# Loading each input tensor of a sequence by one 1.2 MB transfer instead of six 192 KB transfers, in a fused attention and feed-forward kernel

## The chip, the cores and the metric

The kernel runs on one core of a Trainium2 chip. The metric is device time in microseconds (us) of a whole execution, as the median of the runs. The profile is one further execution; its span (first to last instruction) is about 2 us shorter than the time.

Names: TensorE (in the profile PE, and PEld for its weight loads), VectorE (DVE), ScalarE (ACT), GpSimd (POOL), and SyncE (SP), whose queue issues every DMA of this kernel. "L420" is a line of the kernel; the same statement has another number in each variant, so go by the tile names.

## The reference, cut to what matters

```python
# q, k, v, f_logit: (4 sequences, 8 heads, 768 tokens, 48), float32
f = 1 / (1 + exp(-f_logit))
for t in range(768):                       # state: 48 x 48 per head
    state = f[:, :, t, :, None] * state + einsum('bhd,bhe->bhde', k[:, :, t], v[:, :, t])
    y[:, :, t] = einsum('bhd,bhde->bhe', q[:, :, t], state)
x = y.transpose(0, 2, 1, 3).reshape(3072, 384)
out = (maximum(x @ w_in, 0) ** 2) @ w_out  # w_in 384 x 2048, w_out 2048 x 384
```

Each sequence is cut into 6 chunks of 128 tokens, 24 chunks in all. A token's 48 floats of one head (192 bytes) are contiguous in memory; the next token of the head follows, the next head is 768 tokens away. With tokens on partitions every load is therefore made of runs of 192 bytes.

## The kernel before

A small planner inside the program orders all steps: each has an engine, an assumed duration and what it must follow. The result is one fixed order of instructions on each engine. So an instruction whose data is late holds up everything behind it on its engine, even work that is ready.

```python
IOB = 6                                    # six chunk tiles for each of f, k, q, v
LOADS = [0, 1, 2, "i0", "i1", "i2", "i3", 3, 4, 5, "o0", "o1", "o2", "o3"] + list(range(6, NCH))
UNITS = [(0, 2), (2, 1), (3, 1), (4, 1), (5, 1)] + [(c, 3) for c in range(6, NCH, 3)]
...
def load(i):                               # i: chunk; "i0".. and "o0".. are pieces of w_in, w_out
    b, c = divmod(i, NC)
    for n in ("f", "k", "q", "v"):
        def fn(n=n):
            t = io.tile([C, H, D], F32, tag="io_" + n, name="io_" + n)
            nc.sync.dma_start(t, srcs[n][b].rearrange("h s d -> s h d")[c * C:(c + 1) * C])
            st[n, i] = t
        plan.add(f"{n}{i}", "SP", 1.03, fn, take=["io_" + n], rank=0, land=1.9)
```

What follows a load, for chunk i (cut):

```python
a1   ACT   e = exp(-f);  pz = ln(e + 1)            # needs f
p1   PE    pc = ut x pz                            # sums over tokens
a2   ACT   ep = exp(pc);  en = exp(-pc)
v1   DVE   az = k * ep,  q * en                    # needs k, q
p2   PE    tr = transposes of az;   v2: ts = tr
p3   PE    at = ts x ts;            v3: am = at * ut    (DVE)
vc   POOL  vz = v in bf16                          # needs v
p5   PE    ds = az x vz;  s1 DVE tm = ds (+ sz);  s2 POOL sz = tm * en     # state for chunk i + 1
p4   PE    yp = ts x sz + am x vz;  a3: ys = yp;  p6 PE xp = transposes;  v6: xT = xp
mm1  PE    hp = w_in x xT  per unit of 1 to 3 chunks (UNITS);  hr = relu(hp), hT = hr * hr (ACT, DVE)
mm2  PE    op = hT x w_out;  ob = op;  store from the SP queue
```

The buffers pz and az exist twice, so only two chunks can run ahead of the rest. Units of the feed-forward network (FFN) are three chunks wide from chunk 6 on: the FFN of sequence 1 starts when the attention of chunks 6, 7 and 8 is done.

## Time and profile before

The time was 202.44 us (3 runs, 202.26 to 202.61).

| before, from the profile | value |
|---|---|
| TensorE busy | 179.2 of 199.5 us |
| one 192 KB load, issue to issue in the steady state | 1.03 us |
| first cast of v (chunk 0) | 7.20 us |
| first FFN matmul | 19.67 us |
| first FFN matmul of sequence 1 | 70.29 us |

The page of the kernel before, from its parts 1, 2, 3 and 6. The two digit rows are busy tenths in 40 equal slices of the span, the third row is GB/s; the last lines are DMA issues with count, size and median us to landing.

```profile
PE 179.2 (90%) x1824; PEld 122.0 (61%) x1824; DVE 141.7 (71%) x301; ACT 132.2 (66%) x279; POOL 38.6 (19%) x80
...
PE   0667996698989999999999999999999999999973
...
DMA  6999999999999899999989989910111011111111
GB/s 126 192 196 348 318 177 184 252 384 191 207 188 221 192 190 173 230 186 203 208 166 228 212 167 221 164 39 5 39 40 42 0 43 41 39 39 43 39 54 64
DMA packets 107030, 30.19 MB, mean 151 GB/s; under 512 B 100352, under 2 KB 105472, under 8 KB 107008
...
io_f<-in_f_logit_dram SPq DMA_DIRECT2D x24, 192.0 KB, 4.6
...
wi_f<-in_moe_w_in_dram SPq DMA_DIRECT2D x4, 768.0 KB, 8.6
```

The DMA engines are 80%, mostly 90% and more, busy from slice 1 to slice 25 (counted from 0; to 130 us), at some 190 GB/s wherever q, k, v, f are loaded and at up to 384 GB/s in the slices with weights, whose runs are 1.5 to 2 KB. TensorE is at a steady 90% and more only from slice 12 on (60 us). So the early part waits for data and the late part is TensorE's own work.

Stretches of the kernel before: limits and length in us, then busy us (instructions) of PE, PEld, DVE, ACT, POOL, then granted TensorE clock, DMA share, GB/s.

```profile
0.00:71.00 71.00, 56.09 (x692) 42.58 (x693) 55.92 (x114) 46.47 (x93) 19.46 (x45) 1.00 1.05 226
71.00:100.00 29.00, 28.30 (x315) 19.29 (x314) 27.16 (x59) 24.70 (x56) 7.81 (x15) 1.00 1.12 199
100.00:110.00 10.00, 9.72 (x94) 6.25 (x91) 7.78 (x17) 8.12 (x19) 1.98 (x4) 1.00 1.07 197
```

By 71 us TensorE has 56.1 us of work behind it, and is 96% busy from there to the end (123.1 of 128.5 us): at most some 5 us of the time lost before 71 us could be won back.

### The profile page before, as it was taken

To read this page: it belongs to the slowest core of one execution; us is meant where nothing else is said; L and a number is where in the kernel's file an instruction comes from. 1 tells how busy PE (TensorE), PEld (TensorE's weight loads), DVE (VectorE), ACT (ScalarE), POOL (GpSimd) and SP (SyncE) were. 2 spreads that over 40 slices of the span, in tenths; PEclk is the share of its full clock that TensorE was granted. 3 is DMA by queue.
4 is the path that set the end of the run, shared out by engine and by line. 5 is a ranking of instruction groups with operands and counts; after the bars stand their busy time and mean duration, and the time that the engine had idled before them with its cause. 6 is when DMAs were issued, how large, how long until landed. Compare 5 with 4: busy or idle time off the path is not lost.

```text
span 199.5 us, 4771 instructions
## 1 busy us (share of the span) xinstructions
PE 179.2 (90%) x1824; PEld 122.0 (61%) x1824; DVE 141.7 (71%) x301; ACT 132.2 (66%) x279; POOL 38.6 (19%) x80
## 2 busy tenths in 40 slices
PE   0667996698989999999999999999999999999973
PEld 0445785486867666666665666666666665665541
DVE  3569679897799999898987979899755753433200
ACT  4363687696875389769879487787865565555310
POOL 5233011510251323114321211412200200000000
PEclk9999999999999999999999999999999999999999
DMA  6999999999999899999989989910111011111111
GB/s 126 192 196 348 318 177 184 252 384 191 207 188 221 192 190 173 230 186 203 208 166 228 212 167 221 164 39 5 39 40 42 0 43 41 39 39 43 39 54 64
DMA packets 107030, 30.19 MB, mean 151 GB/s; under 512 B 100352, under 2 KB 105472, under 8 KB 107008
## 3 DMA queue, kind: packets, MB, share of 16 engines
q1 hardware_dynamic: 107008, 29.89, 72.5%
q8 instruction: 14, 0.23, 0.5%
q14 instruction: 8, 0.07, 0.1%
HBM read 25.17 MB, written 4.72 MB: 150 GB/s over the span
## 4 chain that ended last, share of the span: by engine, by line
PE 63%; DMA 14%; SPq 10%; ACT 5%; DVE 3%; issue 2%; POOL 1%; DVEq 0%; POOLq 0%; ACTq 0%
PE op L464 26%; PE hp L420 24%; SPq L198 9%; DMA io_f<-in_f_logit_dram 7%; DMA io_v<-in_v_dram 7%; PE tr L312 3%; PE yp L350 3%; PE at L327 2%; PE pc L280 2%; PE xp L364 2%; PE ds L381 1%; ACT pz L270 1%; ACT e L269 1%; ACT ob L474 1%; DVE am L334 1%
## 5 line engine op out<-in xcount | busy, mean ns | idle before, releaser
L420 PE MATMUL hp<-xT,w_in 128*128 128x384 bf16 (+2 forms) x528 | 80.6, 287 | 1.8 <-ACT xT L371 1.3
L464 PE MATMUL op<-w_out,hT 128*128 128x384 bf16 x384 | 77.8, 326 | 2.1 <-ACT ob L474 1.1
L427 ACT ACTIVATE hr<-hp 128x384 bf16<-128x384 f32 (+1 forms) x94 | 47.5, 509 | 23.8 <-PE hp L420 22.7
L420 PEld LDWEIGHTS <-w_in 128*128 128x128 bf16 x528 | 43.3, 99 | 19.7 <-issue 2.1
L436 DVE TENSOR_TENSOR hT<-hr 128x384 bf16<-128x384 bf16 (+1 forms) x91 | 34.3, 378 | 27.5 <-ACT hr L427 26.5
L464 PEld LDWEIGHTS <-hT 128*128 128x128 bf16 x384 | 35.4, 97 | 24.6 <-issue 3.6
L334 DVE TENSOR_TENSOR am<-at,ut 128x512 bf16<-128x512 f32 x48 | 31.7, 682 | 2.2 <-PE at L327 1.9
L398 POOL TENSOR_TENSOR sz<-tm,en 48x192 bf16<-48x192 f32 x40 | 21.9, 549 | 49.6 <-DVE tm L389 30.3
L274 POOL CAST vz<-io_v 128x384 bf16<-128x384 f32 x24 | 13.2, 552 | 66.6 <-DMA io_v<-in_v_dram 39.4
L269 ACT ACTIVATE e<-io_f 128x384 f32<-128x384 f32 x24 | 12.6, 523 | 14.5 <-DMA io_f<-in_f_logit_dram 14.5
L312 PE MATMUL tr<-ident,az 128*128 128x128 bf16 x192 | 16.5, 230 | 2.7 <-DVE az L300 1.6
L300 DVE TENSOR_TENSOR az<-io_k,ep 128x384 bf16<-128x384 f32 x24 | 14.7, 614 | 4.7 <-ACT ep L290 4.6
L429 DVE TENSOR_SCALAR hr<-hp 128x384 bf16<-128x384 f32 (+1 forms) x26 | 15.1, 586 | 2.0 <-PE hp L420 2.0
L434 ACT ACTIVATE hT<-hr 128x384 bf16<-128x384 bf16 (+1 forms) x29 | 15.9, 549 | 0.9 <-DVE hr L429 0.3
L312 PEld LDWEIGHTS <-az 128*128 128x128 bf16 x192 | 12.6, 102 | 6.3 <-DVE az L300 2.4
L474 ACT COPY ob<-op 128x384 f32<-128x384 f32 x18 | 8.6, 477 | 11.4 <-PE op L464 11.3
L280 PE MATMUL pc<-pz,ut 128*128 128x384 bf16 x24 | 8.3, 348 | 8.0 <-ACT pz L270 7.0
L318 DVE COPY ts<-tr 128x1024 bf16<-128x1024 bf16 x20 | 13.7, 684 | 1.6 <-PE tr L312 1.4
L304 DVE TENSOR_TENSOR az<-io_q,en 128x384 bf16<-128x384 f32 x24 | 14.5, 605 | 0.4 <-ACT en L296 0.4
L290 ACT ACTIVATE ep<-pc 128x384 f32<-128x384 f32 x24 | 11.7, 489 | 4.6 <-PE pc L283 4.5
L270 ACT ACTIVATE pz<-e 128x384 bf16<-128x384 f32 x24 | 12.6, 523 | 0.8
L296 ACT ACTIVATE en<-pc 128x388 f32<-128x388 f32 (+1 forms) x24 | 11.9, 494 | 0.0
(40 smaller groups left out, 143.8 us busy)
## 6 DMA issues: line engine op xcount, KB each, us to landing
io_f<-in_f_logit_dram SPq DMA_DIRECT2D x24, 192.0 KB, 4.6
io_k<-in_k_dram SPq DMA_DIRECT2D x24, 192.0 KB, 4.5
io_q<-in_q_dram SPq DMA_DIRECT2D x24, 192.0 KB, 4.5
io_v<-in_v_dram SPq DMA_DIRECT2D x24, 192.0 KB, 4.5
out_dram<-ob SPq DMA_DIRECT2D x24, 192.0 KB, 2.0
wi_f<-in_moe_w_in_dram SPq DMA_DIRECT2D x4, 768.0 KB, 8.6
wo_f<-in_moe_w_out_dram SPq DMA_DIRECT2D x4, 768.0 KB, 7.4
```

Of the source, the lines that this page charges most:

```text
L198: nc.sync.dma_start(t, srcs[n][b].rearrange("h s d -> s h d")[c * C:(c + 1) * C])
L269: nc.scalar.activation(e, st["f", i].rearrange("p h d -> p (h d)"), AFT.Exp, scale=-1.0)
L300: nc.vector.tensor_mul(az[i % 2][:, H:, :D], st["k", i], st["ep", i])
L312: nc.tensor.transpose(tr[:, y, :], a[:, 2 * y:2 * y + 2, :].rearrange("p h d -> p (h d)"), ident)
L334: nc.vector.tensor_mul(t, st["at", i][x], ut4)
L398: nc.gpsimd.tensor_mul(nx[r, :, D * x:D * (x + 1)], st["tm", i][r, :, D * x:D * (x + 1)], st["en", i][r, HD:HD + NP].unsqueeze(2).to_broad ...
L420: nc.tensor.matmul(hp[:, x, :], w_in[:, ks, (f + x) * C:(f + x + 1) * C], xT[:, ks, lo:lo + W], start=(ks == 0), stop=(ks == KS - 1), skip ...
L427: nc.scalar.activation(hr[:, :m, :], st["hp", c0, f][:, :m, :], AFT.Relu)
L429: nc.vector.tensor_scalar_max(hr[:, :m, :], st["hp", c0, f][:, :m, :], 0.0)
L434: nc.scalar.activation(st["hT", g][:, f:f + m, lo:lo + W], hr[:, :m, :], AFT.Square)
L436: nc.vector.tensor_mul(st["hT", g][:, f:f + m, lo:lo + W], hr[:, :m, :], hr[:, :m, :])
L464: nc.tensor.matmul(st["o", i], hT[:, fs, tt * C:(tt + 1) * C], w_out[:, fs, :], start=(fs == 0), stop=(fs == FS - 1))
```

## The change

The intent: 16 large transfers in place of 96 small ones, with fewer issues. Head and chunk strides merge into one dimension (the head stride is six chunk strides), so a whole sequence is one access pattern. All of sequence 0 is loaded, then all weights, then sequences 1, 2, 3. Two large tiles for each tensor take twice the memory of six small ones. The compute engines read slices of the large tiles, with gaps between heads. The planner is told 4.5 us for each large transfer.

```diff
-    IOB = 6
+    IOB = 2
-    LOADS = [0, 1, 2, "i0", "i1", "i2", "i3", 3, 4, 5, "o0", "o1", "o2", "o3"] + list(range(6, NCH))
...
+    LOADS = [0, ("i", 0), ("i", 1), ("i", 2), ("i", 3), ("o", 0), ("o", 1), ("o", 2), ("o", 3), 1, 2, 3]
+    LDUR = 4.5
...
-    def load(i):
-        b, c = divmod(i, NC)
+    def load(b):
         for n in ("f", "k", "q", "v"):
             def fn(n=n):
-                t = io.tile([C, H, D], F32, tag="io_" + n, name="io_" + n)
-                nc.sync.dma_start(t, srcs[n][b].rearrange("h s d -> s h d")[c * C:(c + 1) * C])
-                st[n, i] = t
-            plan.add(f"{n}{i}", "SP", 1.03, fn, take=["io_" + n], rank=0, land=1.9)
+                t = io.tile([C, H, NC, D], F32, tag="io_" + n, name="io_" + n)
+                nc.sync.dma_start(t, srcs[n][b].rearrange("h (c p) d -> p h c d", p=C))
+                for c in range(NC):
+                    st[n, b * NC + c] = t[:, :, c, :]
+            plan.add(f"{n}{b}", "SP", LDUR, fn, take=["io_" + n], rank=0, land=1.9)
...
-        plan.add(f"a1.{i}", "ACT", 1.0, a1, after=[f"f{i}"], take=["pz"], give=[f"io_f:f{i}"])
+        plan.add(f"a1.{i}", "ACT", 1.0, a1, after=[f"f{b}"], take=["pz"])
... (the same for k, q, v; a buffer is given back when its six chunks are used)
```

More of the change, by code (lines that the diff above doesn't have):

```diff
@@ L159 @@
     NCH = B * NC
-    IOB = 6
+    IOB = 2
     WSTB = 4
     HTB = 3
-    LOADS = [0, 1, 2, "i0", "i1", "i2", "i3", 3, 4, 5, "o0", "o1", "o2", "o3"] + list(range(6, NCH))
-    LOADS = [x if isinstance(x, int) else (x[0], int(x[1])) for x in LOADS]
+    LOADS = [0, ("i", 0), ("i", 1), ("i", 2), ("i", 3), ("o", 0), ("o", 1), ("o", 2), ("o", 3), 1, 2, 3]
+    LDUR = 4.5
     UNITS = [(0, 2), (2, 1), (3, 1), (4, 1), (5, 1)] + [(c, 3) for c in range(6, NCH, 3)]
@@ L191 @@
     srcs = {"f": f_logit, "k": k, "q": q, "v": v}
-    def load(i):
-        b, c = divmod(i, NC)
+    def load(b):
         for n in ("f", "k", "q", "v"):
             def fn(n=n):
-                t = io.tile([C, H, D], F32, tag="io_" + n, name="io_" + n)
-                nc.sync.dma_start(t, srcs[n][b].rearrange("h s d -> s h d")[c * C:(c + 1) * C])
-                st[n, i] = t
-            plan.add(f"{n}{i}", "SP", 1.03, fn, take=["io_" + n], rank=0, land=1.9)
+                t = io.tile([C, H, NC, D], F32, tag="io_" + n, name="io_" + n)
[3 more added lines that the diff above has]
+            plan.add(f"{n}{b}", "SP", LDUR, fn, take=["io_" + n], rank=0, land=1.9)
+            use = {"f": "a1", "k": "v1k", "q": "v1q", "v": "vc"}[n]
+            done.append((f"{n}{b}x", [f"{use}.{b * NC + c}" for c in range(NC)], f"io_{n}:{n}{b}"))
+    done = []
     NW = 4
@@ L261, in attention @@
     def attention(i):
-        c = i % NC
+        b, c = divmod(i, NC)
         last = c == NC - 1
@@ L268, in a1 @@
             e = work.tile([C, HD], F32, tag="e", name="e")
-            nc.scalar.activation(e, st["f", i].rearrange("p h d -> p (h d)"), AFT.Exp, scale=-1.0)
+            nc.scalar.activation(e.rearrange("p (h d) -> p h d", d=D), st["f", i], AFT.Exp, scale=-1.0)
             nc.scalar.activation(pz[i % 2][:, :, :D], e.rearrange("p (h d) -> p h d", d=D), AFT.Ln, bias=1.0)
-        plan.add(f"a1.{i}", "ACT", 1.0, a1, after=[f"f{i}"], take=["pz"], give=[f"io_f:f{i}"])
+        plan.add(f"a1.{i}", "ACT", 1.0, a1, after=[f"f{b}"], take=["pz"])
         def vc():
             nc.gpsimd.tensor_copy(vz[i % 3], st["v", i])
-        plan.add(f"vc.{i}", "POOL", 0.52, vc, after=[f"v{i}"], take=["vz"], give=[f"io_v:v{i}"])
+        plan.add(f"vc.{i}", "POOL", 0.52, vc, after=[f"v{b}"], take=["vz"])
         def p1():
@@ L300, in v1k @@
             nc.vector.tensor_mul(az[i % 2][:, H:, :D], st["k", i], st["ep", i])
-        plan.add(f"v1k.{i}", "DVE", 0.5, v1k, after=[f"a2p.{i}", f"k{i}"], take=["az"], give=[f"ep:a2p.{i}", f"io_k:k{i}"])
+        plan.add(f"v1k.{i}", "DVE", 0.5, v1k, after=[f"a2p.{i}", f"k{b}"], take=["az"], give=[f"ep:a2p.{i}"])
         def v1q():
             nc.vector.tensor_mul(az[i % 2][:, :H, :D], st["q", i], st["en", i][:, :HD].rearrange("p (h d) -> p h d", d=D))
-        plan.add(f"v1q.{i}", "DVE", 0.5, v1q, after=[f"a2n.{i}", f"q{i}", f"v1k.{i}"], give=[f"io_q:q{i}"] + ([f"en:a2n.{i}"] if last else []))
+        plan.add(f"v1q.{i}", "DVE", 0.5, v1q, after=[f"a2n.{i}", f"q{b}", f"v1k.{i}"], give=[f"en:a2n.{i}"] if last else [])
         def p2():
@@ L487 @@
         plan.add(f"x{g}", "-", 0, lambda: None, after=users[g], give=[f"xT:v6.{g * GC}"], land=0)
+    for name, after, give in done:
+        plan.add(name, "-", 0, lambda: None, after=after, give=[give], land=0)
     for fn in plan.order():
```

## The prediction

> **What bounds the kernel now.** By the table of stretches TensorE is busy 3.2 to 3.6 of 5 us between 5 and 20 us, about 4.4 of 5 from 20 to 70 us, and 96 to 100% from 70 to 185 us. The DMA queue runs without a gap to about 130 us, at 180 to 220 GB/s wherever it carries q, k, v, f. The chain of waits alternates between DMA and TensorE until an f load lands at 103.7 us; afterwards it is TensorE alone. So only what delays TensorE's start or starves it early is paid; later loads have slack.
>
> **What a load costs.** In the issues view a 192 KB load lands after about 4.5 us, but that is queueing: in the queue's timeline issues settle at one per 1.03 us, and the twelfth load's consumer starts at 15.45 us. That is 1024 runs of 192 B. The change keeps runs of 48 floats. The Trainium skill, "DMA: Bandwidth & Descriptors", rules for kernel authors, says to coalesce small transfers, at least 1 MiB per DMA. I expect that not to help here: transfers already overlap with DMA over 90% busy, while weight pieces with 1.5 to 2 KB runs reach 313 to 384 GB/s. So a 1.2 MB load should take 6 x 1.03 = 6.2 us, against 4.5 us in the new plan. The 80 issues saved were already waiting for the DMA engines.
>
> **What moves.** Before, chunk 0's f, k, q, v arrived at 3.9 to 7.2 us and the first FFN matmul ran at 19.7 us. Estimates for after:
> - f of sequence 0 lands at 9, k at 15, q at 21.5, v at 28 us. Only two chunks can run ahead (pz, az have two buffers): TensorE has 4 us of work before 28.
> - From v through cast, ds, state update, yp of chunk 1, transposes, xT: another 4 to 5 us. First FFN matmul at 32 to 33 us, 13 later.
> - Weights (2.3 us a piece) are in at 46 us, little later than before. Sequence 1's v lands near 71 us; before, chunk 6 was there at 51. Sequence 0 holds about 45 us of TensorE work (179/24 per chunk), so from 33 us it nearly lasts; but the fixed order was planned with v1 near 56 us, so attention of chunks 6 and 7 will hold up TensorE 3 to 4 us.
> - By 71 us TensorE has done about 37 us of work (3 before 33 us, 13 of the next 17 because weight casts crowd VectorE and ScalarE, 20 of the last 21), against 56 before. This deficit, 16 to 20 us, can't be regained: from there before was 96% busy. Sequences 2 and 3 land at 96 and 122 us, long before need.
>
> Strided reads of the big tiles should leave the f32 activations at 522 ns and the multiplies at 550 ns.
>
> **Prediction.** 202.4 + 16.6 = 219 us; 80% range 208 to 229. Faster by over 2%: 0.03; within 2%: 0.04; slower: 0.93.
>
> **What would show it.** First f32 exp on ScalarE at 9 to 10 us; first vz cast on GpSimd at 28; first hp matmul at 31 to 34; packets under 512 B still about 100 thousand; loads 6.2 us apart; sequence 1's first vz cast near 71; TensorE 95% busy from 75 us until the tail; clock 1.0; TensorE busy total 179.
>
> **What would make it wrong.** Large transfers running faster (4.5 us each would give back 6 to 8 us), or slower[...]; order stalls beyond sequence 1, or output stores stuck behind 6 us issues (towards 229); TensorE catching up between 33 and 70 us at above 90% (towards 209).

## More of the kernel before

The timeline of the kernel before (start, us, engine, line, operation, tiles, count): the first v cast and the first FFN matmuls of sequences 0 and 1. Units of two chunks show as 128x256, of three as 128x384.

```profile
7.20 0.50 POOL L274 CAST vz<-io_v 128x384 bf16<-128x384 f32 x1 [3.69 <-DMA io_v<-in_v_dram]
...
19.67 2.72 PE L420 MATMUL hp<-xT,w_in 128*128 128x256 bf16 x12 [0.57 <-ACT xT L371]
...
70.29 1.14 PE L420 MATMUL hp<-xT,w_in 128*128 128x384 bf16 x6
```

## The result, and the profile after

The time is 218.35 us (3 runs, 218.13 to 220.08). The ratio to the kernel before is 1.081 (95% interval 1.0725 to 1.0897). A ratio here is the mean time of one kernel's fast runs over that of the other's fast runs of the same rounds, so it is not quite the ratio of the two medians.

The same lines of the page of the changed kernel:

```profile
PE 177.8 (82%) x1824; PEld 123.0 (57%) x1824; DVE 136.8 (63%) x291; ACT 135.8 (63%) x287; POOL 40.3 (19%) x82
...
PE   0021455999987799996999999999999999999973
...
DMA  5999999999989999997999970100011100101101
GB/s 121 186 186 187 186 330 389 374 237 179 188 172 189 209 187 189 177 184 172 190 191 196 214 178 0 39 36 36 3 38 38 39 25 16 63 28 54 39 36 73
DMA packets 32022, 30.18 MB, mean 139 GB/s; under 512 B 768, under 2 KB 30464, under 8 KB 32000
...
wi_f<-in_moe_w_in_dram SPq DMA_DIRECT2D x4, 768.0 KB, 8.8
...
io_f<-in_f_logit_dram SPq DMA_DIRECT2D x4, 0.2 KB, 9.2
```

(The size of a large issue is shown as 0.2 KB; the bytes in total are the same.) TensorE's busy time is no larger, 177.8 against 179.2 us, so the time was not made by extra work. TensorE's holes are the first slices, a dip at slices 11 to 13, and one at slice 18.

The rate of q, k, v, f did not move: 186 and 187 GB/s in the slices of sequence 0 (1 to 4), where the kernel before has 177 to 196 in slices 1, 2, 5 and 6, with hardly any weights in them. In the SP queue of the changed kernel (start, us, issue) one large issue starts about every 6 us:

```profile
2.08 5.32 SPq L197 DMA_DIRECT2D io_k<-in_k_dram  x1
7.86 5.84 SPq L197 DMA_DIRECT2D io_q<-in_q_dram  x1
14.14 5.78 SPq L197 DMA_DIRECT2D io_v<-in_v_dram  x1
...
56.66 6.90 SPq L481 DMA_DIRECT2D out_dram<-ob  x1
63.77 0.70 SPq L197 DMA_DIRECT2D io_v<-in_v_dram  x1
```

The last two lines show a smaller delay of another kind. The v of sequence 1 is issued behind an output store that stood 6.90 us in the queue, waiting for its result, and the DMA share is 0.46, 0.56 and 0.69 in the three us from 63 to 66. The v of sequence 2 is held in the same way: a store from 83.47 us on for 7.46 us, v at 91.14, DMA share 0.67 and 0.55 in the two 2 us stretches from 90 to 94 (some 1.1 in stretches without such a hole). From these shares I estimate that the two came some 1.5 and 2 us later than the queue alone would have them. No run tested this for the changed kernel; y6 below shows the same on a larger scale.

What did move is when data may be used. The timeline of the changed kernel: first exp, first v cast, first FFN matmul, then the wait at 63 to 73 us with sequence 1's v cast, and the FFN of sequence 1.

```profile
10.04 0.52 ACT L273 ACTIVATE e<-io_f 128x384 f32<-128x384 f32 x1 [8.02 <-DMA io_f<-in_f_logit_dram]
...
28.66 2.00 POOL L278 CAST vz<-io_v 128x384 bf16<-128x384 f32 x4 [25.15 <-DMA io_v<-in_v_dram]
...
37.51 2.76 PE L424 MATMUL hp<-xT,w_in 128*128 128x256 bf16 x12
...
66.49 1.44 PE L424 MATMUL hp<-xT,w_in 128*128 128x128 bf16 x12 [2.40 <-DVE hr L433]
...
72.42 1.41 POOL L278 CAST vz<-io_v 128x384 bf16<-128x384 f32 x3 [15.96 <-DMA io_v<-in_v_dram]
...
88.47 1.14 PE L424 MATMUL hp<-xT,w_in 128*128 128x384 bf16 x6
```

The v of chunk 0 is there at 28.66 instead of 7.20 us, the first FFN matmul runs at 37.51 instead of 19.67, and that of sequence 1 at 88.47 instead of 70.29. This last shift, 18.2 us, is about the difference of the spans (216.6 - 199.5 = 17.1).

Stretches of the changed kernel, to be read against those of before:

```profile
0.00:71.00 71.00, 40.74 (x488) 32.64 (x488) 39.05 (x81) 39.12 (x80) 13.52 (x34) 0.98 0.99 225
71.00:100.00 29.00, 26.91 (x331) 19.32 (x331) 24.57 (x52) 21.18 (x45) 7.72 (x14) 1.00 0.96 186
100.00:110.00 10.00, 8.05 (x98) 5.60 (x98) 6.56 (x15) 7.50 (x18) 4.59 (x9) 1.00 0.98 194
```

TensorE is 15.4 us behind at 71 us (40.7 against 56.1 us of busy time), and loses another 3.1 us from 71 to 110 us (35.0 against 38.0): 1.6 us by 73 us, still at sequence 1, and 1.7 us from 100 to 110 us, at the v of sequence 2.

### The profile page after: what moved, and what is told of

The parts are those of the page before. It is cut to its first block, busy times and chain, and to the rows that moved or that the text cites. A ratio compares the mean times of both kernels' runs of the same rounds, so it can differ in the third digit from the quotient of the medians.

```text
span 216.6 us, 4654 instructions
## 1 busy us (share of the span) xinstructions
PE 177.8 (82%) x1824; PEld 123.0 (57%) x1824; DVE 136.8 (63%) x291; ACT 135.8 (63%) x287; POOL 40.3 (19%) x82
## 4 chain that ended last, share of the span: by engine, by line
PE 66%; DMA 15%; SPq 7%; DVE 5%; ACT 3%; POOL 2%; issue 1%; POOLq 0%; ACTq 0%
PE op L468 26%; PE hp L424 25%; DMA io_v<-in_v_dram 15%; SPq L197 6%; PE tr L316 4%; PE yp L354 3%; PE at L331 3%; PE ds L385 1%; PE pc L284 1%; ACT ob L478 1%; PE xp L368 1%; POOL vz L278 1%; POOL sz L402 1%; DVE hr L433 1%; SPq L481 1%
## 5 line engine op out<-in xcount | busy, mean ns | idle before, releaser
L424 PE MATMUL hp<-xT,w_in 128*128 128x384 bf16 (+2 forms) x528 | 82.7, 291 | 2.4 <-DVE hr L433 2.4
L431 ACT ACTIVATE hr<-hp 128x384 bf16<-128x384 f32 (+1 forms) x95 | 48.5, 513 | 32.7 <-PE hp L424 32.0
L424 PEld LDWEIGHTS <-w_in 128*128 128x128 bf16 x528 | 44.2, 102 | 20.5 <-issue 2.8
L440 DVE TENSOR_TENSOR hT<-hr 128x384 bf16<-128x384 bf16 (+1 forms) x82 | 31.1, 379 | 25.0 <-ACT hr L431 23.8
L316 PE MATMUL tr<-ident,az 128*128 128x128 bf16 x192 | 16.6, 234 | 10.8 <-DVE az L308 5.7
L304 DVE TENSOR_TENSOR az<-io_k,ep 128x384 bf16<-128x384 f32 x24 | 13.4, 564 | 15.2 <-DMA io_k<-in_k_dram 13.9
L438 ACT ACTIVATE hT<-hr 128x384 bf16<-128x384 bf16 (+1 forms) x38 | 20.8, 557 | 0.9 <-DVE hr L433 0.3
L316 PEld LDWEIGHTS <-az 128*128 128x128 bf16 x192 | 13.5, 105 | 13.7 <-DVE az L308 5.9
L362 ACT CAST ys<-yp 128x384 bf16<-128x384 f32 x17 | 8.1, 478 | 17.6 <-PE yp L354 17.4
L308 DVE TENSOR_TENSOR az<-io_q,en 128x384 bf16<-128x384 f32 x24 | 13.7, 575 | 8.2 <-DMA io_q<-in_q_dram 8.2
L478 ACT COPY ob<-op 128x384 f32<-128x384 f32 x19 | 9.1, 478 | 12.7 <-PE op L468 12.6
L287 PEld LDWEIGHTS <-pz 128*128 128x128 bf16 x80 | 5.2, 101 | 13.0 <-issue 11.7
```

The lines of the kernel that those rows point to most:

```text
L308: nc.vector.tensor_mul(az[i % 2][:, :H, :D], st["q", i], st["en", i][:, :HD].rearrange("p (h d) -> p h d", d=D))
L316: nc.tensor.transpose(tr[:, y, :], a[:, 2 * y:2 * y + 2, :].rearrange("p h d -> p (h d)"), ident)
L424: nc.tensor.matmul(hp[:, x, :], w_in[:, ks, (f + x) * C:(f + x + 1) * C], xT[:, ks, lo:lo + W], start=(ks == 0), stop=(ks == KS - 1), skip ...
L431: nc.scalar.activation(hr[:, :m, :], st["hp", c0, f][:, :m, :], AFT.Relu)
L438: nc.scalar.activation(st["hT", g][:, f:f + m, lo:lo + W], hr[:, :m, :], AFT.Square)
L440: nc.vector.tensor_mul(st["hT", g][:, f:f + m, lo:lo + W], hr[:, :m, :], hr[:, :m, :])
```

## The experiments

**Theory.** The size of a transfer as such costs and saves nothing. The loss is the later arrival of usable data: a chunk now waits for the end of four whole transfers. **Rivals**: another DMA rate; the strided reads, two-deep tiles or stores queued behind long issues; the weights placed later; an order of instructions planned with a wrong duration (4.5 us where 6.2 are needed); or the late start alone, or the late sequence 1 alone. Strided reads could be struck off at once in the groups of instructions: the f32 exp has a median of 517 ns (522 before), the multiply by k 549 (554), the v cast 508 (507). A shortage of tiles could be struck off too: in the queue's own waits the loads of the changed kernel waited 0.2 us in all for other engines, those of the kernel before 10.1 us.

All runs in one table. "FFN 0" and "FFN 1" are the starts of the first FFN matmuls of sequences 0 and 1 in the profile, in us.

| run | time | ratio to before, same rounds (95%) | FFN 0 | FFN 1 | span |
|---|---|---|---|---|---|
| before | 202.44 | 1 | 19.67 | 70.29 | 199.5 |
| the change | 218.35 | 1.081 (1.0725 to 1.0897) | 37.51 | 88.47 | 216.6 |
| x1_plan62 | 214.84 | 1.063 (1.0566 to 1.0696) | 36.55 | 86.10 | 214.2 |
| x2_six_in_place | 212.57 | 1.051 (1.0466 to 1.0559) | 38.30 | 84.19 | 211.0 |
| x3_chunk_major | 212.16 | 1.050 (1.0456 to 1.0542) | 37.86 | 82.00 | 210.4 |
| z1_weights_later | 202.87 | 1.003 (0.9978 to 1.009) | 32.03 | 72.85 | 201.5 |
| t1_tensor_major | 207.38 | 1.028 (1.0234 to 1.0319) | 31.49 | 81.92 | 206.3 |
| y1_seq0_chunks | 215.69 | 1.070 (1.0654 to 1.0754) | 19.51 | 87.31 | 213.8 |
| y2_seq1_chunks | 215.73 | 1.071 (1.0646 to 1.0777) | 36.50 | 82.81 | 212.8 |
| y3_seq01_chunks | 203.99 | 1.012 (1.0064 to 1.0179) | 19.50 | 71.20 | 202.3 |
| y1_kept_warm | 216.42 | 1.073 (1.0682 to 1.0769) | 19.37 | 87.15 | 214.4 |
| y6_seq3_large | 207.22 | 1.025 (1.0215 to 1.0275) | 19.61 | 71.94 | 205.3 |
| b1_weights_spread | 201.54, wrong result | 0.998 (0.994 to 1.0014) | 23.58 | 71.12 | 199.1 |
| b1_again, one execution | 203.13, wrong result | none, state unknown | 23.26 | 73.23 | 201.3 |

### x1_plan62: the planner told the true duration

```diff
-    LDUR = 4.5
+    LDUR = 6.2
```

> The changed kernel with one number altered: the planner is told 6.2 us per 1.2 MB load, as measured, in place of 4.5. Data arrives exactly as before. Theory (late arrival of complete sequences is the main cause, the misplanned order a minor one): 211 to 216 us, because tensor work of sequence 0 can now be planned into the hole at 63 to 73 us and the first FFN matmul moves from 37.5 to 32 to 35 us. Rival A (order does not matter at all, arrival alone): 217.5 to 219. Rival B (misplanned order is the main cause): under 208.

Measured: 214.84 us, ratio 1.063 where the change has 1.081. The wrong duration costs 1.8% of the time before, some 3.6 us; the data still comes too late for the rest. TensorE is busy 10.8 of the 11 us from 62 to 73 us (7.0 in the changed kernel), so the hole was planned away, but other waits appeared later. The first FFN matmul moved only to 36.55 us, not to 32 to 35.

### x2_six_in_place: six transfers in the place of one, same plan

```diff
-                t = io.tile([C, H, NC, D], F32, tag="io_" + n, name="io_" + n)
-                nc.sync.dma_start(t, srcs[n][b].rearrange("h (c p) d -> p h c d", p=C))
                 for c in range(NC):
-                    st[n, b * NC + c] = t[:, :, c, :]
+                    t = io.tile([C, H, D], F32, tag="io_" + n, name="io_" + n, bufs=IOB * NC)
+                    nc.sync.dma_start(t, srcs[n][b].rearrange("h s d -> s h d")[c * C:(c + 1) * C])
+                    st[n, b * NC + c] = t
```

> The changed kernel, same plan and same order on every compute engine, but in the place of each 1.2 MB transfer six of 192 KB into six tiles, tensor after tensor (all f, all k, all q, all v of a sequence). Theory (transfer size as such costs and saves nothing; only the arrival of each chunk's four pieces counts): 24 loads still take 24.7 us together, v of chunk 0 lands 5.2 us earlier, near 23.5 us, and the time is 212 to 215. Rival (large transfers move at another rate than small ones): the spacing of the six-load groups differs from 6.2 us by over 5%, and the time moves accordingly.

Measured: 212.57 us, ratio 1.051, as expected. In the SP queue the groups of six small loads start at 5.46, 11.81 and 18.17 us, 6.35 us apart; the large issues started 5.8 to 6.3 us apart while the queue filled, and the consumers of f, k, q, v of sequence 0 start at 10.04, 16.38, 22.64 and 28.66 us, 6.0 to 6.3 us apart. So the rates agree within a few per cent and the large transfer is not slower. The timeline of x2_six_in_place:

```profile
5.46 6.31 SPq L198 DMA_DIRECT2D io_k<-in_k_dram  x6
...
22.80 0.50 POOL L278 CAST vz<-io_v 128x384 bf16<-128x384 f32 x1 [19.28 <-DMA io_v<-in_v_dram]
...
38.30 2.38 PE L424 MATMUL hp<-xT,w_in 128*128 128x256 bf16 x12
...
67.14 0.51 POOL L278 CAST vz<-io_v 128x384 bf16<-128x384 f32 x1 [11.18 <-DMA io_v<-in_v_dram]
```

What six transfers give is that the first of them can be used: v of chunk 0 is cast at 22.80 instead of 28.66 us, that of sequence 1 at 67.14 instead of 72.42, that of sequence 2 at 94.28 instead of 100.30. With the order of the compute engines unchanged, this is worth 3.0%, some 6 us. The gain does not come from sequence 0: the first FFN matmul is no earlier (38.30 against 37.51 us), and by 62 us TensorE has 33.4 us of work behind it against 34.2 in the changed kernel. It comes from 62 to 110 us, at sequences 1 and 2: 45.4 us busy against 41.6.

### x3_chunk_major: chunk after chunk, still the same plan

The edit against x2_six_in_place, cut:

```diff
+                if b < 2 and n != "f":
+                    return
                 for c in range(NC):
-                    t = io.tile([C, H, D], F32, tag="io_" + n, ...)
+                    for m in (("f", "k", "q", "v") if b < 2 else (n,)):
+                        t = io.tile([C, H, D], F32, tag="io_" + m, ...)      # load of tensor m, chunk c
```

> As the run before, but for sequences 0 and 1 the 24 small transfers are issued chunk by chunk (f, k, q, v of chunk 0, then of chunk 1, and so on). Same plan, same order on every compute engine as in the changed kernel; weights arrive when they did there. Theory: v of chunk 0 lands near 7 us, the first FFN matmul is then held by the weights to 31 to 33 us, chunk 6 is complete near 50 us so that the stall at 63 to 73 us goes, and the time is 203 to 207. Rival (the order planned for whole sequences costs the time, whatever arrives): 213 or more.

Measured: 212.16 us. This is a miss: the data of chunk 0 is complete at 7 us, as in the kernel before, but the time is no better than in the run before. The timeline of x3_chunk_major on ScalarE, TensorE and GpSimd shows why:

```profile
16.41 0.52 ACT L276 ACTIVATE e<-io_f 128x384 f32<-128x384 f32 x1 [3.14 <-DMA io_f<-in_f_logit_dram]
...
17.39 0.85 ACT L297 ACTIVATE ep<-pc 128x384 f32<-128x384 f32 x2
...
18.52 0.61 PE L319 MATMUL tr<-ident,az 128*128 128x128 bf16 x4 [8.85 <-DVE az L307]
...
30.88 0.87 POOL L237 CAST w_in<-wi_f 128x512 bf16<-128x512 f32 x1 [5.08 <-DMA wi_f<-in_moe_w_in_dram]
31.72 1.07 POOL L405 TENSOR_TENSOR sz<-tm,en 48x192 bf16<-48x192 f32 x2
...
37.86 2.59 PE L427 MATMUL hp<-xT,w_in 128*128 128x256 bf16 x12
```

The order was planned for f of all six chunks at once: ScalarE has to do the exp of chunks 0 to 3 first and waits for the f of chunk 3 (16.41 us) before it gives chunk 0 its ep. GpSimd has a weight cast (30.88 us, waiting for the weights) ahead of the state update sz, and so the FFN starts at 37.86 us. The Trainium skill ("Perfetto Trace Analysis", per-engine timelines) says that ScalarE, VectorE and GpSimd are strict FIFO; these lines agree. Data that came earlier still was worth nothing more to an order made for late data: arrival and plan have to change together.

### z1_weights_later: the kernel before, with the weights behind all of sequence 0

```diff
-    LOADS = [0, 1, 2, "i0", "i1", "i2", "i3", 3, 4, 5, "o0", "o1", "o2", "o3"] + list(range(6, NCH))
+    LOADS = [0, 1, 2, 3, 4, 5, "i0", "i1", "i2", "i3", "o0", "o1", "o2", "o3"] + list(range(6, NCH))
```

> The kernel before with one edit: all six chunks of sequence 0 are loaded ahead of the weights, as the change does, in transfers of 192 KB. Theory: loading all of sequence 0 before the weights costs a little by itself, 204 to 209 us; the rest of the loss up to 218 comes from merging. Rival (the later weights are the whole loss): 215 to 219.

Measured: 202.87 us, ratio 1.003, a little better than expected. The FFN starts 12 us later (32.03 us), but TensorE does attention meanwhile and is 23.4 of 24 us busy from 38 to 62 us. So a late first FFN matmul alone is not the loss, and the later weights are not either.

### t1_tensor_major: small transfers in the order that the change gives

```diff
-    IOB = 6
+    IOB = 12
-    LOADS = [0, 1, 2, "i0", ... ]
+    LOADS = [0, "i0", "i1", "i2", "i3", "o0", "o1", "o2", "o3", 1, 2, 3]
-    def load(i):
-        b, c = divmod(i, NC)
-        for n in ("f", "k", "q", "v"):
+    def load(b):
+        for n, i in [(n, b * NC + c) for n in ("f", "k", "q", "v") for c in range(NC)]:
```

> The kernel before, transfers of 192 KB with its own plan, but loaded in the order that the change gives: all f, all k, all q, all v chunks of sequence 0, then the weights, then sequences 1, 2, 3 in the same way. With z1_weights_later (chunk after chunk, 202.9) and x1_plan62 (one transfer per tensor, truthful plan, 214.8) it cuts the loss in two. Theory (arrival alone counts): chunk 0's v lands near 23 us instead of 28 and chunk 6's near 66 instead of 72, so 208 to 211; the order of loads costs 5 to 8, waiting for the end of a whole transfer 4 to 7. Rival (only the size of the transfer matters, not the order): 202 to 205.

Measured: 207.38 us, ratio 1.028, slightly under the expected 208 to 211. Together with z1_weights_later and x1_plan62, all three with plans that know the true durations, and with the change itself, it cuts the loss into four steps (differences of the ratios): weights later 0.3%, all f before all k before all q before all v 2.4%, waiting for the end of a whole transfer 3.5%, the wrong duration in the plan 1.8%; in all 8.1%. The third step, measured under the other plan by x2, was 3.0%. These runs stood on several chips and each plan shifts other things too. By the intervals of the ratios alone the first three steps are good to 0.6 to 0.8% and the last to 1.1%: the first is not clear of noise, and the last only just.

### y1, y2, y3: which sequence has to come in chunks

Base is x1_plan62. A sequence is loaded either by large transfers or by slices into the same large tile (cut; in y1 and y3 the weights also go back among the chunks of sequence 0, where the kernel before has them, and y2 leaves them behind sequence 0):

```diff
+    WHOLE = {1, 2, 3}        # y1;  y2: {0, 2, 3};  y3: {2, 3}
+    def load_c(i):
+        b, c = divmod(i, NC)
+        for n in ("f", "k", "q", "v"):
+            def fn(n=n):
+                if c == 0:
+                    st["t" + n, b] = io.tile([C, H, NC, D], F32, tag="io_" + n, name="io_" + n)
+                t = st["t" + n, b]
+                nc.sync.dma_start(t[:, :, c, :], srcs[n][b].rearrange("h (c p) d -> p h c d", p=C)[:, :, c, :])
```

> The changed kernel with the planner told 6.2 us per large load (the run x1_plan62 is its base, 214.8), but sequence 0 loaded chunk by chunk into the same large tiles, with the weights placed among the chunks as in the kernel before; sequences 1, 2, 3 remain large transfers. Theory (two late arrivals in series, each hiding much of the other): TensorE starts as early as before (first FFN matmul near 20 us) but has only some 45 us of work of sequence 0 and then waits for sequence 1's v near 70 us: 210 to 213 us. Rival (the late start alone is the loss): 201 to 205.

> Same base, but sequence 0 one large transfer per tensor and sequence 1 chunk by chunk; sequences 2 and 3 large. Theory: first FFN matmul stays at 36 to 38 us, TensorE then stays busy through 63 to 73 us: 209 to 213 us. Rival (the wait for sequence 1 alone is the loss): 201 to 205.

> Same base, sequences 0 and 1 chunk by chunk in the order of the kernel before, only 2 and 3 by large transfers into tiles read with strides. Theory: both late arrivals are gone and the large transfers that are left cost nothing: 201 to 205 us, ratio to before 0.995 to 1.015. Rival (large transfers, the big tiles' strided reads, the two-deep buffers or stores queued behind 6 us issues cost time wherever they are): over 207.

Measured: y1 215.69, y2 215.73, x1 (both large) 214.84, y3 (both in chunks) 203.99. To mend one of the two late arrivals gave nothing, to mend both gave some 10 us (ratio 1.063 to 1.012). I had expected 2 to 5 us from y1 and 2 to 6 us from y2; both are misses. The two delays are not a sum. The FFN of sequence 1 starts at 86.10 us with both, at 87.31 and 82.81 with one, at 71.20 with none. Over all correct runs the time from there to the end of the span is 124 to 133 us, so where FFN 1 starts, most of the result is settled, though not all: y2 lost more than half of its 3.3 us again by the end (130.0 us from there, x1 128.1).

In y1 TensorE starts early (FFN 0 at 19.51 us), but by 70 us it has used up sequence 0. Its timeline shows the wait for v, and then 12.6 us from the first v cast to the FFN of sequence 1:

```profile
74.73 2.00 POOL L298 CAST vz<-io_v 128x384 bf16<-128x384 f32 x4 [33.66 <-DMA io_v<-in_v_dram]
...
75.29 0.48 PE L405 MATMUL ds<-vz,az 128*128 128x96 bf16 x4 [3.62 <-POOL vz L298]
...
87.31 2.08 PE L444 MATMUL hp<-xT,w_in 128*128 128x384 bf16 x6 [0.61 <-DVE xT L395]
```

In y2 TensorE has 11.2 us of busy time by 38 us (y3: 25.9). From 38 to 100 us it is 95% busy (58.7 of 62 us; y3: 59.8), and so never catches up.

### y1_kept_warm: is it the clock?

After the wait, the stretches of y1_seq0_chunks show TensorE at half clock (the sixth value after the length, 0.50) up to nearly 92 us:

```profile
78.00:80.00 2.00, 1.42 (x19) 1.17 (x20) 1.68 (x3) 1.75 (x5) 1.37 (x3) 0.50 1.11 187
86.00:88.00 2.00, 1.39 (x12) 0.69 (x7) 1.70 (x4) 1.32 (x4) 0.70 (x2) 0.50 1.07 178
92.00:94.00 2.00, 2.00 (x25) 1.32 (x23) 1.83 (x5) 1.17 (x4) 0.26 (x1) 1.00 1.10 181
```

The Trainium skill ("TensorE: Matmul & The Clock Gate", Part 1) says that an idle window of about 3.4 us puts the array's clock to half. This trace agrees: the drop came with an idle time of 3.62 us before the ds matmul at 75.29. The changed kernel's does not: there the clock fell to half at 66 us, within an idle time of 2.40 us. The run fills the hole of y1 with matmuls whose result is overwritten.

```diff
             ds = psum.tile([C, NP, 2 * D], F32, tag="m", bufs=2, name="ds")
+            for _ in range(80 if i == 6 else 0):
+                nc.tensor.matmul(ds[:, 0, :], ident, ident[:, :2 * D], skip_group_check=True)
```

> The run y1_seq0_chunks (215.7 us, granted clock 0.944 to 0.960 in its runs, half clock from 75 to 91 us in its profile) with 80 extra matmuls without use put into the hole where TensorE waits for the first cast of sequence 1's v; their results are overwritten at once. Theory (the wait for sequence 1 costs twice: the hole itself, and some 16 us at half clock after it): the clock stays near 1.0 through 75 to 91 us and the time falls by 3 to 8 us, to 208 to 213. Rival (the half clock costs nothing, because TensorE waits for data there anyway): 215 to 218.

Measured: 216.42 us, no gain; the expectation failed. The stretches of y1_kept_warm:

```profile
78.00:80.00 2.00, 0.93 (x20) 0.78 (x21) 1.80 (x3) 1.62 (x5) 1.21 (x3) 1.00 1.10 197
82.00:84.00 2.00, 1.59 (x19) 1.36 (x20) 2.00 (x5) 0.00 (x0) 0.97 (x2) 0.50 0.63 137
```

The clock now stayed full to 82 us, and yet the FFN of sequence 1 began at 87.15 us, against 87.31. The half clock up to 82 us cost little: from the first v cast to this FFN it is 12.0 us here (75.19 to 87.15) and 12.6 us in y1 (74.73 to 87.31). TensorE is busy about half of the time there (3.0 of 6 us from 76 to 82) and waits for the chain of attention of three chunks through the other engines. From 82 to 92 us the clock fell to half all the same, with TensorE busy 8.9 of 10 us in both runs. Six hp matmuls took 2.08 us there against 1.14 at full clock, so by my estimate up to 4 us of y1's time may be the clock's; no run tests it. By that much y1 may understate what an early sequence 0 alone is worth.

### y6_seq3_large and b1: two more misses

y3 was 1.2% over the kernel before, and its v of sequence 2 was cast only at 103.75 us. So I tried large transfers for sequence 3 alone:

```diff
-    WHOLE = {2, 3}
+    WHOLE = {3}        # and sequence 2 by chunks in LOADS
```

> Only sequence 3 by large transfers, the rest chunk by chunk in the order of the kernel before, all into the large tiles. In y3_seq01_chunks (1.2% over the kernel before) sequence 2's v was cast only at 103.8 us. Theory (a large transfer is free once the TensorE backlog is longer than its own landing): ratio to before 0.997 to 1.006. Rival (large tiles, strided reads or two-deep buffers cost the 1.2%): ratio 1.009 to 1.02.

Measured: 207.22 us, ratio 1.025: slower than y3, a miss. The timeline of y6_seq3_large on SP and VectorE:

```profile
100.87 1.02 SPq L198 DMA_DIRECT2D io_f<-in_f_logit_dram  x1
106.45 2.93 SPq L501 DMA_DIRECT2D out_dram<-ob  x1
109.58 0.72 SPq L198 DMA_DIRECT2D io_k<-in_k_dram  x1
113.88 3.79 SPq L501 DMA_DIRECT2D out_dram<-ob  x1
117.88 0.71 SPq L198 DMA_DIRECT2D io_q<-in_q_dram  x1
...
119.26 0.56 DVE L324 TENSOR_TENSOR az<-io_k,ep 128x384 bf16<-128x384 f32 x1 [3.29 <-DMA io_k<-in_k_dram]
```

Output stores stand between the large loads of the one queue. A store waits for its result, and the next load waits behind it: k is issued 8.7 us after f, q another 8.3 us later. The DMA share falls to 0.68 from 115 to 120 us, v is cast at 133 us (the planner had 123.8), and VectorE, which must take its steps in order, waits 3.29 us for k with the evictions of the FFN behind it. TensorE is busy 17.4 of 20 us from 110 to 130 us, against 20.0 before. This shows 2.6 of the 4.7 us that y6 loses (207.22 against 202.52 in the same rounds); the rest is spread over the run and is not settled.

b1_weights_spread was a try at beating both kernels: the pieces of w_in spread among chunks 3 to 5.

```diff
-    LOADS = [0, 1, 2, "i0", "i1", "i2", "i3", 3, 4, 5, "o0", "o1", "o2", "o3"] + list(range(6, NCH))
+    LOADS = [0, 1, 2, 3, "i0", "i1", 4, "i2", 5, "i3", "o0", "o1", "o2", "o3"] + list(range(6, NCH))
```

> A try at beating the kernel before, chunk transfers kept: the pieces of w_in are spread among chunks 3 to 5, so that TensorE gets attention work earlier, and w_out follows. The kernel's own planner puts it 1.2 us ahead of the kernel before. Theory: 200 to 201.5 us, ratio 0.990 to 0.998. Rival (TensorE is starved by another wait in the first 40 us): 201.5 to 204.

> The kernel b1_weights_spread once more, because its result was wrong (relative error 0.05) although the checks ahead of the chip pass and it differs from the kernel before in the order of loads alone. If the fault lies in the planned order, the same error comes again; if it is an accident of one run, the result is correct.

Measured: 201.54 us, ratio 0.998, and a wrong result, with the same relative error of 0.0497 in both runs. So the fault is not an accident of one run; where it lies was not found. It is no version to use, and it would have gained nothing worth having. No run beat the kernel before.

## Why the prediction was right, point by point

- **The total was right**: 219 predicted, 218.35 measured; 16.6 us of loss predicted, 15.9 measured. The mechanism was right too: the same rate, a later start, a second wait at sequence 1. Some of its parts were off, in both directions, so that the total is right to within 1 us is in part luck.
- **"a 1.2 MB load should take 6 x 1.03 = 6.2 us": right.** The consumers of f, k, q and v of sequence 0 start at 10.04, 16.38, 22.64 and 28.66 us. Coalescing to over 1 MB, which the Trainium skill advises ("DMA: Bandwidth & Descriptors", rules for kernel authors), did not raise the rate (186 and 187 GB/s), as predicted. The prediction's reason, runs that stay at 192 bytes, fits the up to 389 GB/s of the weights, but no run changed the length of the runs alone.
- **"packets under 512 B still about 100 thousand": wrong.** They fell from 100,352 to 768. The class from 512 B to 2 KB rose from 5,120 to 29,696, by 24,576, which is a quarter of the 98,304 runs: four runs of 192 bytes now share a packet. The rate stayed, so the number of packets was not what limited it.
- **"Another 4 to 5 us ... First FFN matmul at 32 to 33 us": mis-sized.** From v (28.66) to the first FFN matmul (37.51) it took 8.9 us. GpSimd casts four chunks of v and a piece of w_in before it comes to the first state update at 31.20 us, and the planned order puts another chunk's transposes ahead of the FFN.
- **"13 of the next 17 ... 20 of the last 21", 37 us of work by 71 us: mis-sized the other way.** TensorE was 100% busy from 38 to 62 us, and had done 40.7 us by 71. The two errors nearly cancel. And while sequence 1 is late anyway, an earlier or later start of sequence 0 changes little, as y1 shows.
- **"attention of chunks 6 and 7 will hold up TensorE 3 to 4 us": right.** The two waits are 2.40 us (66.49) and 1.57 us (72.98). Not foreseen was the clock of 0.56 to 0.59 from 66 to 70 us behind the first.
- **"This deficit, 16 to 20 us, can't be regained" and "TensorE 95% busy from 75 us until the tail": right.** The deficit was 15.4 us at 71 us and 16.9 at 73, when the wait for sequence 1 was over (its v was cast at 72.42, predicted near 71). From 75 to 200 us TensorE was 98% busy.
- **"Sequences 2 and 3 land at 96 and 122 us, long before need": wrong for sequence 2.** Its v was cast at 100.30 us, by the estimate above in part because its load stood behind an output store, and TensorE stood still 1.95 us at it: 8.05 of 10 us busy from 100 to 110 us. For the v of sequence 3 nothing waited.
- **Strided reads, TensorE's busy total (179 predicted, 177.8) and the mean clock (0.992): right.**
- The prediction added the late start and the late sequence 1 into one balance at 71 us. In y1 and y2 each alone cost about the whole, with the open question of y1's clock. That it was not a sum did not matter for the number, but it would have for anybody who mended only one.

## What to carry to other kernels

A transfer is a unit of waiting as well as a unit of moving. Here DMA was already kept busy and the runs in memory stayed as short as they were: merging transfers saved nothing, and every consumer waited for the last byte of the merged one. Look at which chunk's last piece starts the first work of the busiest engine, and order the loads for that. When two delays end at the same join, mend both before you judge either; and in a kernel with fixed orders, plan again whenever arrivals change. Where one queue carries loads and stores, look at what stands in front of a late load.

## What the Trainium skill lacked or had wrong

- "DMA: Bandwidth & Descriptors", rules for kernel authors: coalescing is advised without regard to when the data can be used. (Of the other side, "Perfetto Trace Analysis" says under "DMA Optimizations" that splitting DMAs may let some start sooner, and may shorten the whole if the DMA engines are generally idle.) Here DMA was 90% and more busy, the merged transfer had the same rate (186 and 187 GB/s, consumers 6.0 to 6.3 us apart, against 6 x 1.03 us) and cost 3.0% by itself (x2 against the change).
- The same page, "Why small descriptors are slow": it says that putting consecutive descriptors into one packet saves a fixed cost of each packet and is worth it up to 256 B. Here four runs of 192 bytes went into one packet (24,576 packets for 98,304 runs) with no gain in rate. Nor does it say that an access pattern of a whole sequence is packed in this way and one of a chunk is not.
- "TensorE: Matmul & The Clock Gate", Part 1: for the drop to half clock it gives the length of one idle window, about 3.4 us; that frequent short idle times can do it too it says further down, without a length. In the changed kernel the clock fell within an idle time of 2.40 us (66 us). In y1_kept_warm it fell to 0.50 at 82 us although TensorE was busy 0.93 and 0.97 us of the two 2 us stretches before and the longest wait that the timeline shows there is 1.19 us.
